# Pooled attention feeding a ResMLP block: GpSimd's v sum put behind VectorE's, scores ahead of v's product, unread products at the start, token products earlier

## The chip, the cores and the metric

The kernel runs on one core of a Trainium2 chip. The metric is device time in microseconds (us) of one execution, the median of several runs. Now and then a run falls into a slower state with a lower granted clock (381.28 us at 0.95 in one run below, where the other five took 369.5 to 371.52 us); the times and ratios compared below are of the other runs, called fast, unless a line says otherwise.

A *lead* is by how much sooner a step starts after the change than before. *Unread products* are products of a tile of zeros whose result nothing reads. Names: PE is TensorE's products and PEld its weight loads, DVE is VectorE, ACT is ScalarE, POOL is GpSimd, SP is the engine that issues most loads. L409 is line 409 of the kernel that ran. The changed kernel has some more lines at its top, so the sum of v is at L409 and L411 before and at L415 and L417 after; v's product with the selection matrix is L417 before and L423 after.

## The reference

```python
# q, k, v: (8 batches, 8 heads, 576, 64); pool = 8
k_p, v_p = mean of k, v over groups of 8 rows            # 72 rows
attn = softmax(q @ k_p.T / sqrt(64))
x = heads side by side of attn @ v_p                     # (8, 576, 512)
# ResMLP with affine steps
a1 = alpha1 * x + beta1
u  = x + lam * (w_tok @ a1)
ch = relu((alpha2 * u + beta2) @ w_ch1) @ w_ch2          # 512 -> 2048 -> 512
out = u + lam * ch
```

## The kernel before

The program is written out in order; each engine runs its own instructions in that order and waits for what it needs. The 36 chunks of 128 rows (8 batches of 4.5 chunks) form 9 blocks of four chunks for the MLP. While block n runs its MLP on TensorE, the attention of batch n + 1 is threaded between its products. The first batch has nothing to hide behind: loads, attention, token products and MLP follow each other. These parts matter here (cuts are marked):

```python
def sum_v(b, u, eng=nc.vector):              # pool v by 8: three adds, 128x512, 128x256, 128x128
    t = st1[b]["v"][u]
    for n in (4, 2):
        eng.tensor_tensor(out=t[:, :, 0:n], in0=t[:, :, 0:n], in1=t[:, :, n:2 * n], op=ALU.add)
    vs = work.tile([P, 2, D], F16, tag="v_sum", bufs=2, name="v_sum")
    eng.tensor_tensor(out=vs, in0=t[:, :, 0], in1=t[:, :, 1], op=ALU.add)
    ...
# att_V(b, u): product of the sums with a selection matrix (ps_v), then two copies into vp
# att_S(b, h): two score products (ps_sc) and their exponentials on ScalarE (ET)
# att_AV(b, h): five products with v (ps_av), reciprocal, and x written by VectorE
# att_X(b, h0, h1, eng): xs = x * lam * alpha1
# mix_T(b, c): token product of chunk c (ps_tok), then u and u_bf on VectorE
# mix_uT(key): transposes of u_bf (ps_uT), copied to u_fm by ScalarE: the MLP's input

sum_v(0, 0)                                  # first batch: VectorE sums heads 0-3 ...
att_Vrem(0, nc.scalar.copy)
sum_v(0, 1, nc.gpsimd)                       # ... and GpSimd heads 4-7, at the same time
att_S(0, 4)
att_V(0, 0, nc.vector.tensor_copy)
att_AV(0, 0)
att_S(0, 5)
att_AV(0, 1)
att_AV(0, 2)
att_X(0, 0, 2, nc.gpsimd)
att_S(0, 6)
...
def attention(b):                            # later batches: (place among the MLP's steps, what)
    ...
    for c in range(5):
        at = 25.4 + 0.8 * c if late else 25.0 + (0.8 if b % 2 else 1.0) * c
        todo.append((at, lambda c=c: mix_T(b, c)))
        if c < 4 or b % 2:
            key = (b, c) if c < 4 else (b - 1, 4)
            todo.append((at + 1.8, lambda key=key: mix_uT(key)))
# mlp_B(n, m, part), four w2 products each, stands at places 16 to 31
```

The softmax here doesn't subtract the row's maximum and nothing guards it: scores larger than these inputs give would overflow.

## Time and profile before

| | before |
|---|---|
| time, median of 3 runs | 372.29 us (372.1 to 372.67) |
| span of the profiled run | 370.5 us |
| TensorE busy | 353.9 us (95%) |
| first token product starts | 27.28 us |
| TensorE's waits after 40 us | three for u_bf, 0.8 us in all |

The page cuts the span into 40 slices of 9.26 us; a digit is the busy share in tenths. These are TensorE's and the loads' rows of the kernel before:

```profile
PE   6589999999999999999999999999999999999995
DMA  6999795049002902093107402470100002002002
```

TensorE is short of work in the first three slices alone (6, 5, 8), which are the loads, the attention and the first token products of the first batch. From there it is at 9 until the last slice. So there are two places to gain: the first 28 us, and small waits elsewhere that add to tenths of a microsecond.

### The profile page before, as it was taken

Reading aid. Unit: us, or ns where it says so; the run is one execution under the profiler, and the core shown is the slowest. Engines: PE = TensorE matmul, PEld = TensorE weight load, DVE = VectorE, ACT = ScalarE, POOL = GpSimd, SP = SyncE. Lnnn points to the kernel's source line nnn. Section 1 sums busy time; section 2 is a strip of 40 time slices with the busy share of each in tenths; the row PEclk is TensorE's granted clock in tenths of the full one; section 3 lists DMA queues with packets and bytes.
Section 4 is the critical chain, followed back from the end, with each engine's and each line's share of the span. In section 5 each row is a group of like instructions: output and inputs, shape, how many; then the busy total and the mean of one; then the engine's idle time right before and its main releaser. Section 6 shows DMA issues by size and latency. Waiting matters only on the chain.

```text
span 370.5 us, 6098 instructions
## 1 busy us (share of the span) xinstructions
PE 353.9 (95%) x2302; PEld 196.0 (53%) x2344; DVE 217.5 (59%) x426; ACT 201.9 (54%) x408; POOL 145.7 (39%) x188
## 2 busy tenths in 40 slices
PE   6589999999999999999999999999999999999995
PEld 2366655455545554455545555555455545544544
DVE  7876355773697358833885289527963687643011
ACT  3763984269614981399228932795159704712710
POOL 8955907910494038601880079105920410000000
PEclk9999999999999999999999999999999999999999
DMA  6999795049002902093107402470100002002002
GB/s 247 269 224 328 186 271 183 2 145 350 31 30 80 333 30 58 28 315 98 58 28 253 160 31 58 156 257 30 57 28 2 28 31 58 2 28 85 2 30 83
DMA packets 19575, 43.27 MB, mean 117 GB/s; under 512 B 2193, under 2 KB 4565, under 8 KB 19546
## 3 DMA queue, kind: packets, MB, share of 16 engines
q1 hardware_dynamic: 17488, 37.89, 30.2%
q0 software_dynamic: 1888, 4.86, 6.9%
q8 instruction: 18, 0.29, 0.3%
q10 hardware_dynamic: 170, 0.14, 0.2%
q14 instruction: 11, 0.09, 0.1%
HBM read 38.30 MB, written 9.44 MB: 129 GB/s over the span
## 4 chain that ended last, share of the span: by engine, by line
PE 84%; DVE 7%; ACT 3%; DMA 2%; issue 2%; SPq 1%; ACTq 0%
PE ps_h L542 32%; PE ps_ch L565 31%; PE ps_tok L511 9%; PE ps_sc L446 4%; DVE u_bf L515 3%; PE ps_av L463 2%; DVE u_sb L513 2%; DMA qk_raw<-in_k_dram 2%; PE ps_uT L526 2%; PE ps_q L362 2%; DVE v_u L409 1%; ACT wtT L284 1%; ACT Hj L547 1%; PE ps_kp L394 1%; SPq L78 1%
## 5 line engine op out<-in xcount | busy, mean ns | idle before, releaser
L542 PE MATMUL ps_h<-u_fm,w 128*128 128x512 bf16 (+1 forms) x574 | 133.2, 373 | 1.2 <-ACT u_fm L528 0.4
L565 PE MATMUL ps_ch<-w,Hj 128*128 128x512 bf16 x493 | 123.4, 379 | 1.1 <-issue 0.2
L547 ACT ACTIVATE Hj<-ps_h,bias_cols 128x512 bf16<-128x512 f32 x144 | 96.6, 690 | 36.5 <-PE ps_h L542 21.4
L542 PEld LDWEIGHTS <-w 128*128 128x128 bf16 x592 | 64.8, 114 | 47.9 <-issue 0.6
L477 POOL TENSOR_TENSOR xs<-x_tm,lamal_bc 128x512 bf16<-128x512 f32 x24 | 30.5, 1271 | 140.1 <-DVE x_tm L470 137.1
L565 PEld LDWEIGHTS <-Hj 128*128 128x128 bf16 x592 | 55.6, 98 | 48.1 <-issue 0.2
L528 ACT COPY u_fm<-ps_uT 128x512 bf16<-128x512 bf16 x36 | 21.1, 585 | 88.3 <-PE ps_uT L526 88.3
L448 ACT ACTIVATE ET<-ps_sc 128x288 f16<-128x288 f32 (+1 forms) x128 | 51.7, 487 | 15.8 <-PE ps_sc L446 15.6
L511 PE MATMUL ps_tok<-xs,wtT 128*128 128x512 bf16 (+1 forms) x197 | 48.3, 379 | 0.2
L401 DVE CAST kpT<-ps_kp 64x288 bf16<-64x288 f32 x31 | 14.1, 455 | 52.0 <-PE ps_kp L397 51.6
L572 DVE TENSOR_TENSOR u_sb<-u_sb,ps_ch 128x512 f32<-128x512 f32 (+1 forms) x37 | 24.9, 673 | 24.9 <-PE ps_ch L565 23.8
L515 DVE TENSOR_TENSOR u_bf<-u_sb,al_bc 128x512 bf16<-128x512 f32 (+1 forms) x39 | 34.4, 881 | 1.4
L571 DVE TENSOR_TENSOR ps_ch<-lam_bc,ps_ch 128x512 f32<-128x512 f32 x32 | 22.1, 692 | 20.6 <-PE ps_ch L565 20.4
L513 DVE TENSOR_TENSOR u_sb<-x_tm,ps_tok 128x512 f32<-128x512 f32 (+1 forms) x40 | 27.4, 684 | 10.5 <-PE ps_tok L511 10.0
L132 POOL TENSOR_TENSOR qk_raw<-qk_raw 128x512 f32<-128x512 f32 (+1 forms) x28 | 32.6, 1165 | 1.1
L470 DVE TENSOR_TENSOR x_tm<-ps_av,rec 128x320 f32<-128x320 f32 x64 | 31.5, 492 | 2.7
L511 PEld LDWEIGHTS <-wtT 128*128 128x128 bf16 (+1 forms) x200 | 19.3, 98 | 22.7 <-PE ps_vec L271 0.3
L468 DVE RECIPROCAL rec<-ps_av 128x5 f32<-128x5 f32 x64 | 12.3, 193 | 32.0 <-PE ps_av L466 31.9
L446 PE MATMUL ps_sc<-qT,kpT 128*128 128x288 bf16 (+1 forms) x128 | 28.8, 306 | 0.6 <-DVE kpT L401 0.5
L463 PEld LDWEIGHTS <-ET 72*128 72x128 f16 (+1 forms) x256 | 16.7, 100 | 14.2 <-DVE vp L421 0.6
L409 DVE TENSOR_TENSOR v_u<-v_u 128x512 f32<-128x512 f32 (+1 forms) x30 | 19.7, 657 | 0.8
L463 PE MATMUL ps_av<-vp,ET 72*128 72x66 f16 (+1 forms) x256 | 18.6, 196 | 0.5 <-DVE vp L421 0.4
(112 smaller groups left out, 302.6 us busy)
## 6 DMA issues: line engine op xcount, KB each, us to landing
qk_raw<-in_q_dram SPq DMA_DIRECT2D x16, 512.0 KB, 5.6
qk_raw<-in_k_dram SPq DMA_DIRECT2D x16, 512.0 KB, 7.5
v_u<-in_v_dram SPq DMA_DIRECT2D x32, 256.0 KB, 6.7
out_dram<-u_sb SPq DMA_DIRECT2D x32, 256.0 KB, 2.3
w<-in_moe_w_ch_dram POOLq DMA_DIRECT2D x2, 1024.0 KB, 11.6
w<-in_moe_w_ch_dram POOLq DMA_DIRECT2D x4, 512.0 KB, 10.8
rem_raw<-in_q_dram SPq DMA_DIRECT2D x8, 128.0 KB, 5.3
rem_raw<-in_k_dram SPq DMA_DIRECT2D x8, 128.0 KB, 5.5
```

The lines of the kernel that those rows point to most:

```text
L132: eng.tensor_tensor(out=t[:, :, 0:n], in0=t[:, :, 0:n], in1=t[:, :, n:2 * n], op=ALU.add)
L446: nc.tensor.matmul(out=ps_sc[0:n, 0:288], lhsT=kpT_pool[u][:, j, r, 72 * hh:72 * hh + n], rhs=st["qT"][u][:, h % 4, :])
L448: nc.scalar.activation(out=ET[0:n, 64 + j:64 + S + j:2], in_=ps_sc[0:n, 0:288], func=AF.Exp, bias=0.0, scale=1.0 / 64)
L463: nc.tensor.matmul(out=av[:, c, :], lhsT=ET[:, m0:m0 + 256:2], rhs=vp1)
L470: nc.vector.tensor_tensor(out=x[:, :, dd:dd + D], in0=av[:, :, 0:64], in1=rec.unsqueeze(2).to_broadcast((P, 5, D)), op=ALU.mult)
L477: eng.tensor_tensor(out=xs[:, 0:4, cols], in0=x[:, 0:4, cols], in1=lamal_bc[:, cols].unsqueeze(1).to_broadcast((P, 4, D * (h1 - h0))), op= ...
L511: nc.tensor.matmul(out=ps_tok, lhsT=wtT[0:kk, at, t0:t0 + P], rhs=xs[0:kk, sc, :], start=(sc == 0), stop=(sc == 4))
L513: nc.vector.tensor_tensor(out=s["u"][p0:p1, :], in0=st1[b]["x"][p0:p1, c, :], in1=ps_tok[p0:p1, 0:DM], op=ALU.add)
L515: eng.tensor_tensor(out=s["u_bf"][p0:p1, :], in0=s["u"][p0:p1, :], in1=al2_bc[p0:p1, :], op=ALU.mult)
L542: nc.tensor.matmul(out=ps_h[:, t0:t1], lhsT=w1_of(cc, j), rhs=u_fm[n][:, cc, t0:t1], start=(cc == 0), stop=(cc == 3))
L547: nc.scalar.activation(out=t, in_=ps_h, func=AF.Relu, bias=bias_cols[:, j:j + 1], scale=1.0)
L565: nc.tensor.matmul(out=ps, lhsT=Hj[n, j][:, 128 * m:128 * m + 128], rhs=w2_of(n, j, cols), start=(j == 0), stop=(j == NJ - 1))
```

## The change

Its intent: let VectorE sum its v without GpSimd beside it, give ScalarE two more scores to work on before v's product, raise TensorE's clock with unread products, and start the later token products a little earlier. The diff, cut to its core (`keep_warm(n)` issues n unread products; it was also moved up, and its left operand is now a part of `warm` instead of the identity):

```diff
+    warm = const.tile([P, DM], BF, tag="warm", name="warm")   # moved up
+    nc.vector.memset(warm, 0.0)                               # was GpSimd's
...
     new_batch(1)
+    keep_warm(6)
     ps_lam = broadcast(0)
     nc.scalar.copy(out=lam_bc, in_=ps_lam)
+    keep_warm(2)
     ps_lamal = broadcast(1)
...
-    keep_warm(2)
...
+    v_00 = st1[0]["v"][0]
     sum_v(0, 0)
     att_Vrem(0, nc.scalar.copy)
+    nc.gpsimd.memset(v_00[:, 0, 0, 0:1], 0.0)
     sum_v(0, 1, nc.gpsimd)
     att_S(0, 4)
+    att_S(0, 5)
     att_V(0, 0, nc.vector.tensor_copy)
     att_AV(0, 0)
-    att_S(0, 5)
     att_AV(0, 1)
+    att_S(0, 6)
+    att_X(0, 0, 2, nc.gpsimd)
     att_AV(0, 2)
-    att_X(0, 0, 2, nc.gpsimd)
-    att_S(0, 6)
+    att_S(0, 7)
     att_AV(0, 3)
     att_X(0, 2, 4, nc.gpsimd)
-    att_S(0, 7)
...
-            at = 25.4 + 0.8 * c if late else 25.0 + (0.8 if b % 2 else 1.0) * c
+            at = 25.2 + 0.8 * c if late else 24.6 + (0.8 if b % 2 else 1.0) * c
```

The memset writes one column of a tile that VectorE has finished with. Its only use is that GpSimd may write this tile only after VectorE's sum has read it, and so waits.

More of the change, by code (lines that the diff above doesn't have):

```diff
@@ L62, with keep_warm @@
     NBLK = len(chunks) // 4
+    def keep_warm(count):
+        ps = gp("ps_warm")
+        for _ in range(count):
+            nc.tensor.matmul(out=ps, lhsT=warm[:, 0:P], rhs=warm)
     st1 = {}
@@ L216 @@
     xs_pool = consts([P, 5, DM], BF, "xs", 2)
-    warm = const.tile([P, DM], BF, tag="warm", name="warm")
     b2c_bf = const.tile([P, 4], BF, tag="b2c_bf", name="b2c_bf")
@@ L245, in fill_mix @@
         nc.gpsimd.memset(wtT[:, :, S:640], 0.0)
-        nc.gpsimd.memset(warm, 0.0)
         nc.gpsimd.memset(xs_pool[1][0:64, 4, :], 0.0)
@@ L495, in chunk_of @@
         return key, st2[key]
-    def keep_warm(count):
-        ps = gp("ps_warm")
-        for _ in range(count):
-            nc.tensor.matmul(out=ps, lhsT=identity_bf, rhs=warm)
     def mix_T(b, c, eng=nc.vector):
```

## The prediction

> **What bounds the kernel now.** I read the page first (busy shares, chain of waits by engine), then TensorE's waits over the whole span, then the timeline of each engine from 10 to 28 us, and last the end of one steady block (137 to 156 us).
>
> The page, busy shares and chain by engine:
>
> ```profile
> PE 353.9 (95%) x2302; PEld 196.0 (53%) x2344; DVE 217.5 (59%) x426; ACT 201.9 (54%) x408; POOL 145.7 (39%) x188
> PE 84%; DVE 7%; ACT 3%; DMA 2%; issue 2%; SPq 1%; ACTq 0%
> ```
>
> TensorE is the bound: 353.9 of 370.5 us, so all its idle time is 16.6 us. Only that can be saved, because the change removes no work that is read later. TensorE's waits, the whole span (waiter, released by: us in total, times, longest):
>
> ```profile
> PE ps_v L417 <- DVE v_sum L411: 3.5, 1, 3.5
> PE ps_bc L260 <- DMA vecs<-in_moe_lam_dram: 2.7, 1, 2.7
> PE ps_uT L526 <- DVE u_bf L515: 0.8, 3, 0.3
> PE ps_rs L293 <- ACT wtT L284: 0.6, 1, 0.6
> ```
>
> The largest is the target: v's product of the first batch (line 417) waits 3.5 us for VectorE's sum of v. The 0.8 us in three pieces is the only recorded wait of size after 40 us. The timeline there, VectorE first, then GpSimd (start, duration, both us):
>
> ```profile
> 14.84 2.57 DVE L409 TENSOR_TENSOR v_u<-v_u 128x512 f32<-128x512 f32 x1
> ...
> 15.56 2.44 POOL L409 TENSOR_TENSOR v_u<-v_u 128x512 f32<-128x512 f32 x2
> 18.07 0.52 POOL L411 TENSOR_TENSOR v_sum<-v_u 128x128 f16<-128x128 f32 x1
> ```
>
> and the same three VectorE instructions in the second batch, with GpSimd quiet, then ScalarE's first exponential after its long pause:
>
> ```profile
> 47.17 1.15 DVE L409 TENSOR_TENSOR v_u<-v_u 128x512 f32<-128x512 f32 x2
> 48.36 0.29 DVE L411 TENSOR_TENSOR v_sum<-v_u 128x128 f16<-128x128 f32 x1
> ...
> 20.19 0.83 ACT L448 ACTIVATE ET<-ps_sc 128x288 f16<-128x288 f32 x2 [3.50 <-PE ps_sc L446]
> ```
>
> The reader is to see three things. VectorE's first-heads sum runs from 14.84 to 18.75 us, 3.9 us, while GpSimd sums the second heads; alone it takes 48.65 - 47.17 = 1.5 us. GpSimd is hardly hurt (1.30 us for its 128x512, against 1.27 us for its other 128x512 adds of two inputs). And ScalarE idles 3.5 us, because the scores of head 5 stand behind the first product with v in TensorE's order.
>
> **What the Trainium skill says.** "SBUF — State Buffer", section "Who interferes with whom": a VectorE instruction with two SBUF inputs contends with a GpSimd instruction that reads SBUF, the later one blocked until the first is done. The trace agrees on the contention (2.57 us against 0.69 us for a 128x512 sum), but not simply on who was first: VectorE's add started 0.72 us ahead of GpSimd's. In those 0.72 us GpSimd issued the second load of w1 (14.79 to 15.56), so descriptor writing may hold the port too. "GPSIMD Engine Reference", section "Engine selection": two-input elementwise work is about twice as slow on GpSimd; here 1.30 against 0.69 us. "TensorE: Matmul & The Clock Gate", Part 1: TensorE runs at half clock until about 3.4 us of sustained work. The page's clock row says 9 all along, yet four products with v take 0.22 us in the chain at 20.39 and 0.12 us at 53.24, so the early stage does run at half rate.
>
> **The change, part by part.**
>
> 1. GpSimd waits for VectorE (a one-column memset of the tile that VectorE sums). VectorE's sum then costs 1.5 us from 14.8: done at 16.3 if the load's descriptors do not block it, and at about 15.56 + 1.5 = 17.05 if they do. I take the middle, 16.7, against 18.75: 2.05 us earlier. GpSimd's sum starts only then and takes 1.3 + 0.75 + 0.5 = 2.5 us, plus 0.1 for the memset: done at 19.3, against 18.6 before. Before, that result was first used at 22.2, so it had slack.
>
> 2. Scores of head 5 go ahead of v's product, and those of heads 6 and 7 one product earlier. ScalarE does head 5's exponentials (0.83 us) in its pause, after 16.7. Before, from VectorE's sum (18.75) to head 6's exponential (21.30) took 2.55 us, with head 5's 0.83 us of ScalarE inside; now about 1.4 us.
>
> 3. From there two chains run to the first token product, which started at 27.28. ScalarE's: four exponentials 1.5, copies of v 0.5, then four copies of the transposed token weights and the row sums (22.68 to 27.10 before with the copies of v, 4.4 us): 16.7 + 1.4 + 1.5 + 4.4 + 0.2 = 24.2. GpSimd's: its sum at 19.3, then three products x times lam*alpha, each 1.27 + 0.45 us, 5.2 us: 24.5, and some 0.2 for VectorE's own one beside it. So the first token product goes to about 24.6: **2.7 us earlier**; 3.1 with the early VectorE end, 2.3 with the late one. GpSimd becomes the tighter of the two.
>
> 4. Unread products at the beginning: six of 128x512, then two between the two broadcasts, in place of two later ones; the clear of their input goes from GpSimd (0.53 us) to VectorE. TensorE waited 2.7 us for lam then, so the six lie mostly in idle time (6 x 0.43 = 2.6 us cold, from about 1.2 to 3.8), and delay the first broadcast by 1.1 us at most. The second-half k load, used by VectorE at 11.28, sets the pace until 14.8. I count **0 to -0.2 us**: faster k products on the chain, and a warm array for the first products with v, which the GpSimd chain mostly hides.
>
> 5. mix_T of later batches at 24.6 for 25.0 (25.2 for 25.4 in the first block). The order of instructions shows where this lands. In even batches nothing but the token products moves; the last transposes keep their place. In the first block the last transposes keep their place too. In batches 3, 5 and 7 the last transpose moves ahead of one group of w2 products (0.86 us), which before filled the time in which VectorE finished. The end of such a block:
>
> ```profile
> 152.32 0.69 DVE L513 TENSOR_TENSOR u_sb<-x_tm,ps_tok 64x512 f32<-64x512 f32 x1
> 153.04 1.06 DVE L515 TENSOR_TENSOR u_bf<-u_sb,al_bc 64x512 bf16<-64x512 f32 x1
> ...
> 154.16 0.40 PE L526 MATMUL ps_uT<-identity_bf,u_bf 128*128 128x128 bf16 x4 [0.29 <-DVE u_bf L515]
> ```
>
> VectorE is busy almost without a gap from 144.38 to 154.10, and was held by TensorE only 0.34 us at its start. If the token products start 0.86 us earlier, VectorE gains at most 0.33, and perhaps nothing, because its first u_bf then still waits for GpSimd's k sum that began at 144.38. TensorE is 0.86 us earlier at the last transpose and waits: 0.29 + 0.86 - 0.33 = 0.8 to 1.15 us in place of 0.29. That **costs 0.5 to 0.9 us** in each of batches 3 and 5, and some 0.2 in batch 7, where GpSimd has no next batch: together about 1.5 us.
>
> Sum: -2.7 - 0.1 + 1.5 = -1.3 us; 372.29 - 1.3 = **371.0 us**.
>
> **Rivals.**
> - *The serial GpSimd becomes the bound of the start.* Its sum now follows VectorE's, and its three products follow. For it: the chain above ends later than ScalarE's. Against a large loss: before, it also worked without a break from 21.57 to 26.56 and the first token product started 0.7 us later. If VectorE is blocked by the descriptors, the gain at the start falls to 2.3 us: 371.4 us.
> - *The steady part gains.* Earlier token products may give VectorE a head start that removes the three waits (0.8 us), if GpSimd's contention falls differently. Then 372.29 - 2.8 - 0.8 = 368.7. Against it: VectorE is already full there, and the changed order takes its filler away.
> - *The gain at the start is swallowed by loads.* The DMA share is about 1.0 from 9 to 37 us, so starting the second batch's loads earlier does not make them land earlier. Against it: GpSimd's casts and sums of the second batch, and VectorE's v sum at 41.35, show no wait for a DMA. The last v of that batch is issued at 33 and lands some 6.6 us later, its first half by 37.6, and VectorE would want that at 38.6. If it does bite, up to 1 us is lost: 372.
> - *The early unread products get in the way*: if the array is still cold at the broadcasts, the second ends at 8.8 instead of 7.6 us and the first exponentials come 0.5 us later; ScalarE's pause of 3.5 us takes that up.
>
> **Range and chances.** Start gain 1.9 to 3.4 us, steady loss -0.5 to 2.2 us: a change between -3.9 and +0.3 at the corners; both are unlikely to be at their ends at once, so 369.4 to 372.1 us should hold it 8 times in 10. The 2% bound is 7.4 us. All idle time that the change touches is smaller, and nothing in it adds 7 us of work, so within 2% is nearly certain.
>
> **What would show it right or wrong.** Right: TensorE's wait at line 417 falls from 3.5 to about 1.5 us; VectorE's three v sums take 1.5 to 2.3 us and GpSimd's start after them; ScalarE's pause ahead of head 6 falls under 1 us; the first token product starts near 24.6; TensorE's waits for u_bf grow from 0.8 to about 2.2 us, in batches 3 and 5. Wrong: VectorE's sum still takes 2.5 us or more with GpSimd still (then the load's descriptors, or the data's arrival, held it and not GpSimd's sum), a first token product after 25.5, a DMA wait at the second batch, or u_bf waits that vanish.

## The result and the profile after

The changed kernel took 371.49 us (median of 4 runs, 371.15 to 371.97) against 372.2 us of the kernel before (4 runs). The ratio is 0.9983, with a 95% interval of 0.9964 to 1.0003. A ratio here is the mean time of one kernel's fast runs over that of the other's of the same rounds, so it is not quite the ratio of the two medians. That is 0.7 us by the medians; since the interval includes 1, no gain is shown by the times.

The page of the changed kernel, busy shares and chain by engine:

```profile
PE 357.2 (97%) x2308; PEld 196.4 (53%) x2350; DVE 217.1 (59%) x427; ACT 201.8 (55%) x408; POOL 147.3 (40%) x188
PE 89%; DVE 5%; ACT 4%; issue 1%; DVEq 0%
```

TensorE's busy time rose by 3.3 us although the span fell: unread products, 4.16 us of it after and 1.45 before, count as busy. A busy share is no measure of use.

TensorE's waits in the changed kernel, over the span (waiter, released by: us in total, times, longest):

```profile
PE ps_uT L526 <- DVE u_bf L515: 2.1, 5, 0.6
PE ps_warm L68 <- DVE warm L160: 1.3, 1, 1.3
PE ps_sc L452 <- ACT qT L389: 0.8, 1, 0.8
PE ps_rs L299 <- ACT wtT L290: 0.6, 1, 0.6
PE ps_v L423 <- DVE v_sum L417: 0.6, 1, 0.6
```

The large wait for VectorE's v sum is gone: 0.6 us for 3.5. The wait for u_bf, which had been 0.8 us in three pieces, is now the largest. The timeline of the changed kernel's first batch (start, duration, engine, what; in brackets the idle time before it and what ended it):

```profile
15.32 1.15 DVE L415 TENSOR_TENSOR v_u<-v_u 128x512 f32<-128x512 f32 x2
...
16.51 0.29 DVE L417 TENSOR_TENSOR v_sum<-v_u 128x128 f16<-128x128 f32 x1
...
16.86 0.10 POOL L613 MEMSET v_u<- 128x1 f32 x1 [1.34 <-DVE v_sum L417]
16.96 2.07 POOL L415 TENSOR_TENSOR v_u<-v_u 128x512 f32<-128x512 f32 x2
...
18.59 1.60 ACT L454 ACTIVATE ET<-ps_sc 72x288 f16<-72x288 f32 x4 [0.37 <-PE ps_sc L452]
...
24.79 3.41 PE L511 MATMUL ps_tok<-xs,wtT 128*128 128x512 bf16 x15
```

VectorE's three adds take 1.48 us (15.32 to 16.80) where they took 3.9. GpSimd's start after them. ScalarE pauses 0.37 us ahead of head 6 where it had paused 3.5 us ahead of head 5. The first token product starts at 24.79 us, 2.5 us earlier. What it waited for at the end, from the chain that ended last in the changed kernel:

```profile
20.62 1.96 ACT wtT L290 x3
...
23.04 0.70 ACT wtT L290
...
23.78 0.44 PE ps_rs L299 x5
```

These are ScalarE's copies of the transposed token weights and the products behind them, to which TensorE adds an unread product that ends at 24.69 us. VectorE's own product with lam*alpha ends at 24.65 us. GpSimd's third one of 128 rows had ended at 24.09 us; from 19.5 us on no GpSimd instruction stands in this chain.

The end of the block of batch 3 in the changed kernel, TensorE's timeline:

```profile
149.09 0.39 PE L526 MATMUL ps_uT<-identity_bf,u_bf 128*128 128x128 bf16 x4
149.87 0.40 PE L526 MATMUL ps_uT<-identity_bf,u_bf 128*128 128x128 bf16 x4 [0.40 <-DVE u_bf L515]
150.32 0.81 PE L565 MATMUL ps_ch<-w,Hj 128*128 128x512 bf16 x3
151.69 0.40 PE L526 MATMUL ps_uT<-identity_bf,u_bf 128*128 128x128 bf16 x4 [0.55 <-DVE u_bf L515]
151.92 1.89 PE L565 MATMUL ps_ch<-w,Hj 128*128 128x512 bf16 x8
153.65 2.54 PE L542 MATMUL ps_h<-u_fm,w 128*128 128x512 bf16 x11
```

Two transposes now wait, 0.95 us together, and eight w2 products (1.7 us) that could have filled the time stand behind the last of them. Before, the order was: a w2 group, the third transpose, a group, the fourth, a group, the last, one more group. So the fourth and the last have each overtaken one group of four. The last u_bf of the same block in the changed kernel, which the last transpose waits for:

```profile
150.57 1.06 DVE L515 TENSOR_TENSOR u_bf<-u_sb,al_bc 64x512 bf16<-64x512 f32 x1
```

VectorE ends it at 151.63 us, against 154.10 before: 2.47 us earlier, which is the lead that the block began with. The earlier token products have not made VectorE finish any sooner. The last transpose follows it at once in both kernels, but from its start to the next block it was 1.10 us before (154.16 to 155.26, one group) and is 1.96 us now (151.69 to 153.65, two groups): 0.86 us more.

Where the gain of the start goes can be read off by lining up the first w1 product (L542) of each block in the two traces:

| block starts, us | 1 | 2 | 3 | 4 | 5 | 6 | 7 | end of span |
|---|---|---|---|---|---|---|---|---|
| before | 77.10 | 115.94 | 155.26 | 194.11 | 233.42 | 272.28 | 311.12 | 370.5 |
| after | 74.60 | 113.47 | 153.65 | 192.52 | 232.69 | 271.56 | 310.56 | 369.9 |
| lead | 2.50 | 2.47 | 1.61 | 1.59 | 0.73 | 0.72 | 0.56 | 0.6 |

The lead of 2.5 us falls by 0.86 us at the end of batch 3's block, by 0.86 us at the end of batch 5's, and by 0.16 us at batch 7's. It does not change in the blocks of the even batches.

### The profile page after: what moved, and what is told of

The parts are those of the page before. It is cut to its first block, busy times and chain, and to the rows that moved or that the text cites. A ratio compares the mean times of both kernels' runs of the same rounds, so it can differ in the third digit from the quotient of the medians.

```text
span 369.9 us, 6111 instructions
## 1 busy us (share of the span) xinstructions
PE 357.2 (97%) x2308; PEld 196.4 (53%) x2350; DVE 217.1 (59%) x427; ACT 201.8 (55%) x408; POOL 147.3 (40%) x188
## 4 chain that ended last, share of the span: by engine, by line
PE 89%; DVE 5%; ACT 4%; issue 1%; DVEq 0%
PE ps_h L542 32%; PE ps_ch L565 30%; PE ps_tok L511 11%; PE ps_sc L452 4%; PE ps_av L469 2%; PE ps_q L368 2%; DVE u_bf L515 2%; PE ps_uT L526 2%; DVE u_sb L513 1%; PE ps_warm L68 1%; PE ps_bc L266 1%; ACT wtT L290 1%; ACT qT L372 1%; DVE xs L483 1%; ACT Hj L547 1%
## 5 line engine op out<-in xcount | busy, mean ns | idle before, releaser
L542 PE MATMUL ps_h<-u_fm,w 128*128 128x512 bf16 (+1 forms) x574 | 133.7, 373 | 1.4 <-ACT u_fm L528 0.4
L542 PEld LDWEIGHTS <-w 128*128 128x128 bf16 x592 | 64.8, 114 | 47.9 <-issue 0.6
L571 DVE TENSOR_TENSOR ps_ch<-lam_bc,ps_ch 128x512 f32<-128x512 f32 x32 | 22.1, 691 | 24.8 <-PE ps_ch L565 24.7
L515 DVE TENSOR_TENSOR u_bf<-u_sb,al_bc 128x512 bf16<-128x512 f32 (+1 forms) x39 | 35.2, 902 | 1.4
L511 PEld LDWEIGHTS <-wtT 128*128 128x128 bf16 (+1 forms) x200 | 18.3, 98 | 21.4 <-DVE xs L483 2.6
L469 PEld LDWEIGHTS <-ET 72*128 72x128 f16 (+1 forms) x256 | 16.7, 100 | 14.1 <-DVE vp L427 0.6
L415 DVE TENSOR_TENSOR v_u<-v_u 128x512 f32<-128x512 f32 (+1 forms) x30 | 18.6, 621 | 1.5 <-DMA v_u<-in_v_dram 0.7
```

Of the source, the lines that this page charges most:

```text
L469: nc.tensor.matmul(out=av[:, c, :], lhsT=ET[:, m0:m0 + 256:2], rhs=vp1)
L511: nc.tensor.matmul(out=ps_tok, lhsT=wtT[0:kk, at, t0:t0 + P], rhs=xs[0:kk, sc, :], start=(sc == 0), stop=(sc == 4))
L515: eng.tensor_tensor(out=s["u_bf"][p0:p1, :], in0=s["u"][p0:p1, :], in1=al2_bc[p0:p1, :], op=ALU.mult)
L542: nc.tensor.matmul(out=ps_h[:, t0:t1], lhsT=w1_of(cc, j), rhs=u_fm[n][:, cc, t0:t1], start=(cc == 0), stop=(cc == 3))
```

## The experiments

Twelve runs were made, in three groups of four; each group had its own runs of the kernel before on the same chip (medians 371.98, 372.59 and 372.44 us). All results were correct. Each ratio is to the kernel before. By the 2% rule all twelve are "same"; the differences below are smaller and rest on the intervals and the traces.

| label | what it is | median, us | ratio (95%) |
|---|---|---|---|
| start_1and2 | before + GpSimd's wait + order of scores | 369.76 | 0.9945 (0.9928 to 0.9962) |
| mix_only | before + earlier token products | 374.3 | 1.0061 (1.0045 to 1.0078) |
| warm_only | before + early unread products | 373.02 | 1.0021 (1.0005 to 1.0037) |
| after_mix_back | changed kernel, token products put back | 370.03 | 0.9950 (0.9936 to 0.9963) |
| part1_wait | before + GpSimd's wait | 369.8 | 0.9936 (0.9917 to 0.9955) |
| part2_order | before + order of scores | 371.96 | 0.9994 (0.9976 to 1.0013) |
| after_uT_kept | changed kernel, transposes put back | 370.04 (fast runs; 370.28 with the slow one) | 0.9945 (0.9923 to 0.9967) |
| after_warm_ones | changed kernel, ones in the unread products | 372.35 | 0.9997 (0.9980 to 1.0014) |
| start_again | start_1and2 once more | 369.82 | 0.9929 (0.9911 to 0.9947) |
| uT4_deferred | start_1and2, last transpose later | 368.26 | 0.9900 (0.9874 to 0.9927) |
| no_unread | start_1and2 without any unread product | 369.79 | 0.9928 (0.9906 to 0.9951) |
| after_warm_long | changed kernel, 16 early products for 6 | 372.44 | 1.0000 (0.9977 to 1.0024) |

### The reordered first batch alone (start_1and2, start_again)

```diff
 # on the kernel before
+    v_00 = st1[0]["v"][0]
     sum_v(0, 0)
     att_Vrem(0, nc.scalar.copy)
+    nc.gpsimd.memset(v_00[:, 0, 0, 0:1], 0.0)
     sum_v(0, 1, nc.gpsimd)
 # and att_S(0, 5) to att_S(0, 7), att_X(0, 0, 2) in the order of the changed kernel
```

> The kernel before with only the reordered first batch: GpSimd waits for VectorE's v sum, and the scores of head 5 to 7 go earlier; no early unread products, token products of later batches where they were. My theory: the start gives 2.5 to 3 us and the early unread products gave nothing, so the first token product starts at 24.2 to 25.0 us (27.28 before), u_bf waits of TensorE stay at 0.8 us, and the time is 369.3 to 369.8 us. VectorE's v sum starts near 14.84 us, while GpSimd still issues the loads of w1 (until 15.56): if descriptor writing blocks it, the three v sums take about 2.2 us; if only GpSimd's own sum did, 1.5 us. Rival: the early unread products are what made the start faster: then the first token product is at 26 us or later and the time at 371 us or more.

It took 369.76 us, and 369.82 us when it ran again: 2.0 and 2.6 us under the kernel before by the ratios. The u_bf waits stayed at 0.8 us. The first token product started at 25.08 us, at the slow edge of what I expected, because the whole start was late in this run: VectorE's adds began at 15.61 us, since the load of k landed later. It settles whether the writing of load descriptors holds VectorE up. The timeline of start_1and2:

```profile
15.56 0.77 POOL L317 DMA_DIRECT2D w<-in_moe_w_ch_dram  x1
15.61 1.15 DVE L409 TENSOR_TENSOR v_u<-v_u 128x512 f32<-128x512 f32 x2
```

VectorE's first two adds took 1.15 us, which is their time alone, although GpSimd issued the second load of w1 through 0.72 us of it. Descriptor writing did not block them.

For the second time, as a base:

> The kernel with only the reordered first batch once more, as the base for the two next runs on the same chip: 2.0 to 2.6 us under the kernel before, u_bf waits 0.8 us in three pieces.

That held: 0.9929, and u_bf waits of 0.8 us in three pieces. In this trace, unlike the changed kernel's, the chain to the first token product runs through GpSimd's sum of v (16.33 to 19.04 us).

### The earlier token products alone (mix_only)

```diff
 # on the kernel before
-            at = 25.4 + 0.8 * c if late else 25.0 + (0.8 if b % 2 else 1.0) * c
+            at = 25.2 + 0.8 * c if late else 24.6 + (0.8 if b % 2 else 1.0) * c
```

> The kernel before with only the token products of later batches earlier (24.6 and 25.2 for 25.0 and 25.4). My theory: the start is as before (first token product at 27.3 us), TensorE's waits for u_bf grow from 0.8 to about 2.1 us, and the time grows by 1.7 to 2.0 us, to about 374 us. Rival: the earlier token products are neutral or gain, and the missing gain of the change was lost elsewhere: 371.5 to 372.3 us with u_bf waits under 1 us.

The time rose by 0.61%, 2.3 us, somewhat more than expected, and the interval (1.7 to 2.9 us) holds the 1.9 us that the table of leads shows. TensorE's waits in mix_only have the line of the changed kernel:

```profile
PE ps_v L417 <- DVE v_sum L411: 2.9, 1, 2.9
...
PE ps_uT L526 <- DVE u_bf L515: 2.1, 5, 0.6
```

The first token product started at 27.55 us (27.28 before). The loss is made by this part, without help from the start.

### The early unread products alone (warm_only)

```diff
 # on the kernel before
+    keep_warm(6)
     ps_lam = broadcast(0)
     nc.scalar.copy(out=lam_bc, in_=ps_lam)
+    keep_warm(2)
     ps_lamal = broadcast(1)
...
-    keep_warm(2)
```

> The kernel before with only the early unread products (six and two at the beginning in place of two later). My theory: the second broadcast ends 1.4 us later, the first exponentials 0.8 us later and VectorE's v sum 0.3 to 0.5 us later; the array stays cold, so the first token product moves to 27.6 to 27.8 us and the time grows by 0.3 to 0.5 us, to about 372.6 us. Rival: they warm the array by 10 us (score products start to start 0.12 us apart rather than 0.24 us), and the first token product is at 27.0 us or earlier.

The time rose by 0.21% (0.2 to 1.4 us), and the first token product started at 27.96 us. TensorE's timeline of warm_only shows why nothing was gained:

```profile
8.97 1.03 PE L368 MATMUL ps_q<-identity_bf,q_bf 128*128 128x128 bf16 x8
...
11.27 1.35 PE L452 MATMUL ps_sc<-qT,kpT 128*72 128x288 bf16 x4 [0.81 <-ACT qT L389]
```

Eight transposes took 1.03 us, as they did in the kernel before, so the array was at half rate still; they started at 8.97 us, against 7.54 before. The scores then waited 0.81 us for ScalarE's copy of q. How much the early products cost in the whole is not settled. In this trace the second half of k was also late (VectorE waited for it until 12.02 us, 11.28 before). The time rose by 0.21%, but after_mix_back, which has them, and start_1and2, which has not, differ by only 0.05% on the same chip.

### Token products put back (after_mix_back)

```diff
 # on the changed kernel
-            at = 25.2 + 0.8 * c if late else 24.6 + (0.8 if b % 2 else 1.0) * c
+            at = 25.4 + 0.8 * c if late else 25.0 + (0.8 if b % 2 else 1.0) * c
```

> The changed kernel with the token products of later batches put back where they were. My theory: the first token product stays at 24.8 us, the u_bf waits fall back from 2.1 to 0.8 us, and the time is 1.7 to 2.0 us under the changed kernel's, about 369.6 us. Rival: the gain of the start is given back anyhow in the steady part (loads, or VectorE): 371 us or more.

370.03 us, a ratio of 0.9950, with u_bf waits of 0.8 us. The first token product started at 25.15 us, not at 24.8. So with the gain of the start in place the loss of the token products can be taken back, and the start's gain arrives at the end.

### GpSimd's wait alone (part1_wait) and the order of scores alone (part2_order)

```diff
 # part1_wait: on the kernel before
+    nc.gpsimd.memset(v_00[:, 0, 0, 0:1], 0.0)
     sum_v(0, 1, nc.gpsimd)
 # part2_order: on the kernel before, only att_S(0, 5) to att_S(0, 7) and att_X(0, 0, 2) moved
```

> The kernel before with GpSimd's wait alone; scores of head 5 stay behind the first product with v. My theory: VectorE's three v sums take 1.5 us instead of 3.9, the product with v starts some 2 us earlier, but head 5's exponentials still come after it, so the first token product moves by about 1.7 us only (25.4 to 25.7 us against 27.28) and the time by -1.5 to -1.9 us, near 370.3 us. Rival: the wait does nothing by itself, because GpSimd's sum, started later, holds the second heads' product: first token product after 26.5 us, 371.5 us or more.

It gained more than I expected: 0.64%, 2.4 us by the ratio, and the first token product started at 24.52 us. The timeline of VectorE in part1_wait:

```profile
14.49 1.15 DVE L409 TENSOR_TENSOR v_u<-v_u 128x512 f32<-128x512 f32 x2
15.68 0.29 DVE L411 TENSOR_TENSOR v_sum<-v_u 128x128 f16<-128x128 f32 x1
```

The adds took 1.48 us, 2.4 us less than before. From their end (15.97) to the first token product (24.52) it was 8.55 us, against 8.53 us before (18.75 to 27.28). So the chain behind the sum is as long as it was, and the whole of what VectorE saves reaches the token products.

> The kernel before with the scores of heads 5, 6 and 7 earlier, but GpSimd and VectorE still summing side by side. My theory: TensorE's wait for VectorE's v sum stays near 3 us, head 5's exponentials (0.83 us) move into ScalarE's pause, and the first token product comes 0.8 to 1.1 us earlier (26.2 to 26.5 us), the time -0.7 to -1.0 us, near 371.1 us. Rival: the order alone gives nothing, since GpSimd's products with lam*alpha or VectorE end last: within 0.3 us of the kernel before.

The ratio is 0.9994: no gain is shown. Of the expected 0.7 to 1.0 us (0.9981 to 0.9973) the smaller is inside the interval, the larger outside. The trace has the first token product at 26.26 us, as expected, but 0.65 us of this 1.0 us comes from VectorE's sum, which ended earlier although GpSimd still worked beside it. ScalarE's timeline in part2_order:

```profile
16.12 1.49 ACT L448 ACTIVATE ET<-ps_sc 72x288 f16<-72x288 f32 x4
19.89 1.60 ACT L448 ACTIVATE ET<-ps_sc 72x288 f16<-72x288 f32 x4 [2.28 <-PE ps_sc L446]
```

Head 5's exponentials did move ahead of the pause, and the chain from the end of VectorE's sum (18.10) to the token product is 8.16 us, 0.4 us shorter. That is less than the 0.83 us moved. In the changed kernel and in start_1and2 it is 7.99 us; in start_again, the same program as start_1and2, 8.57 us, and in after_mix_back 8.42 us. So the order is worth 0 to 0.55 us in single traces, and the times don't resolve it: part1_wait alone is as fast as start_1and2.

### Transposes put back (after_uT_kept)

```diff
 # on the changed kernel
-                todo.append((at + 1.8, lambda key=key: mix_uT(key)))
+                todo.append((at + (2.0 if late else 2.2), lambda key=key: mix_uT(key)))
```

> The changed kernel with its early token products, but each transpose of u put back where it was (offset 2.2 and 2.0 for 1.8). My theory: the loss comes from the last transpose having overtaken its filler of four w2 products, so the u_bf waits fall from 2.1 to under 1 us and the time to 369.5 to 370.0 us, as with everything put back. Rival: the early token products themselves cost, by making VectorE and GpSimd collide more: u_bf waits stay above 1.5 us, or the waits move elsewhere, 371 us or more.

The ratio of the fast runs is 0.9945, the same as with everything put back. So early token products do no harm by themselves that the time shows; it was the place of the transposes. This run puts the fourth and the last back together and doesn't separate them. The profile of this kernel fell in the slow state (381 us, granted clock 0.95), so its waits are not read here, and the expected fall of the u_bf waits is not shown directly.

### The last transpose later still (uT4_deferred)

```diff
 # on start_1and2
-                todo.append((at + 1.8, lambda key=key: mix_uT(key)))
+                todo.append((at + 1.8 if c < 4 else 31.5, lambda key=key: mix_uT(key)))
```

In an odd batch the fifth chunk, (b - 1, 4), belongs to a later block than the next one. Its transpose may stand behind the last w2 products.

> The reordered first batch alone, and in odd batches the last transpose of u goes behind the last group of w2 products (it is not needed by the next block). My theory: the place of the last transpose against its filler is what makes the u_bf waits, so the three waits (0.8 us) vanish and the time falls by 0.6 to 0.9 us against the run of the reordered first batch alone. Rival: the waits move to the copies of u or to the next block's first products, and the time stays within 0.2 us.

368.26 us, a ratio of 0.9900, against 0.9929 of start_again on the same chip: about 1.1 us better, somewhat more than expected, though the two intervals overlap. The traces agree: the starts of the blocks gain 0.32, 0.48 and 0.47 us on start_again at the ends of the blocks of batches 1, 3 and 5, and nothing at the end of batch 7's. The list of TensorE's waits has no line for u_bf any more, and TensorE's busy time from 80 to 240 us rose from 159.36 of 160 us (start_again) to 159.94. This version is faster than both kernels, by 1.0% than the kernel before.

### What the unread products do (after_warm_ones, after_warm_long, no_unread)

```diff
 # after_warm_ones: on the changed kernel
-    nc.vector.memset(warm, 0.0)
+    nc.vector.memset(warm, 1.0)
 # after_warm_long: on the changed kernel
-    keep_warm(6)
+    keep_warm(16)
 # no_unread: on start_1and2, both remaining pairs removed
-    keep_warm(2)
...
-    keep_warm(2)
```

> The changed kernel with ones instead of zeros in the unread products. In the changed kernel TensorE was busy from 1.3 to 10 us and yet the products until 20 us ran at half rate. Theory A: zero operands don't count as activity for the clock; with ones the second broadcast takes 1.0 instead of 2.0 us, score products stand 0.12 instead of 0.24 us apart from about 6 us on, and the first token product starts by 24.5 us. Theory B: the value doesn't matter, the early stage is cold for another reason (these forms of products, or gaps): everything within the spread of the changed kernel, first token product 24.6 to 25.1 us, 371.5 us.

The value did not matter to the clock there: the broadcasts took 2.07 us each and the first scores stood as far apart as with zeros. The time was that of the kernel before (0.9997); the first token product started at 25.36 us, outside what either theory named, with VectorE's sum late by 0.16 us.

> The changed kernel with 16 unread products at the beginning in place of six, 6.9 us at half rate. Theory A: sustained full-size products release the clock within 3.4 to 6.8 us, so that the later of them stand 0.22 us apart instead of 0.43 and the score products after them 0.12 us instead of 0.24 us apart; the broadcasts end later, near 10 us, and the first token product is at 25 us or a little later. Theory B: nothing in this stage releases the clock: all 16 stand 0.43 us apart, the broadcasts end at 13 us, the first scores come 4 us later, and the time grows by 2 to 4 us.

TensorE's timeline of after_warm_long:

```profile
1.32 5.32 PE L68 MATMUL ps_warm<-warm 128*128 128x512 bf16 x16 [1.32 <-DVE warm L160]
6.57 1.12 PE L266 MATMUL ps_bc<-vecs,ones_row 1*128 1x512 f32 x2
...
9.21 0.62 PE L368 MATMUL ps_q<-identity_bf,q_bf 128*128 128x128 bf16 x8
...
12.21 1.06 PE L368 MATMUL ps_q<-identity_bf,q_bf 128*128 128x128 bf16 x8
```

Theory A held as to the clock: sixteen products in 5.3 us cannot all have stood 0.43 us apart (6.9 us), the broadcasts took 1.1 us for 2.07, and eight transposes 0.62 us for 1.03. But at 12.21 us the same eight transposes took 1.06 us again, and the kernel's time is that of the kernel before (1.0000). The rate was won and lost again before the part of the start where it could help, and that part waits for loads, VectorE and ScalarE anyway.

> The reordered first batch alone with no unread products at all (both pairs removed). My theory: unread products do nothing for the clock in the first 20 us, and the pair ahead of the token products only fills a wait for ScalarE: within 0.3 us of the reordered first batch alone, first token product 7.9 to 8.4 us after the product with v, as there. Rival: they keep the array's clock up, and the token products then start cold: TensorE's 15 token products take 6 us in place of 3.4 and the time grows by 1 us or more.

369.79 us and 0.9928, as start_again (0.9929). The 15 token products took 3.41 us with or without unread products ahead of them. They do nothing that the time shows. The trace has the first token product at 23.58 us, 8.0 us after the sum's end, as expected, but 1.3 us earlier than start_again's (24.84). That run took 368.56 us, the fastest of the six; whether the missing products or chance made its start so early, one trace doesn't tell.

## Why the prediction was right

The time on record was 371.0 us with a range of 369.4 to 372.1; 371.49 us was measured. By its steps:

1. **VectorE's sum.** It said 1.5 us if descriptors do not block, 2.2 us if they do, and took the middle. It is 1.48 us, and start_1and2 shows the adds at full speed beside a load being issued. Half of this hedge was wrong. The sum's end, 16.7 in the prediction and 16.80 in the trace, came out right partly by luck: the adds also started 0.48 us later than before (15.32 for 14.84). That GpSimd was hardly hurt before holds for its first add alone (1.30 us, 1.27 alone); its second took 1.06 us, and 0.73 alone.
2. **The order of scores.** Counted as part of a step from 2.55 to 1.4 us. The changed kernel needed 1.8 us there (16.80 to 18.59), and the order alone shortened its chain by 0.4 us in one trace. This term was too large; part1_wait shows that GpSimd's wait brings nearly all of the start's gain.
3. **The two chains to the first token product.** 24.6 us predicted, 24.79 measured; GpSimd's sum ended at 19.57 (19.3 predicted). But which chain is the tighter was wrong: GpSimd's third product of 128 rows was done at 24.09, while ScalarE's and TensorE's chain, predicted for 24.2, and VectorE's own product ended near 24.7. That the number fits is in part luck. ScalarE paused 0.37 us (under 1 predicted). TensorE's wait for v's sum is 0.6 us, not 1.5: its products ahead of this one now end 0.96 us later (16.28 for 15.32), 0.58 us because they start later and 0.38 us by head 5's scores, which I had forgotten.
4. **Early unread products.** Predicted 0 to -0.2 us. They did not raise the clock, and no gain is seen: two comparisons put their cost at 0.05% and 0.21% (0.2 and 0.8 us), of which the first is within the noise. The prediction's own rival came true: with the array still cold the second broadcast ended at 9.03 us (7.60 before) and the first exponentials started at 11.70 us (10.91 before).
5. **The later token products.** This step carries the result. Predicted: the last transpose overtakes a group of w2 products in batches 3, 5 and 7, at 0.5 to 0.9 us each for the first two and 0.2 us for the third, and nothing in even batches or in the first block. The leads fall by 0.86, 0.86 and 0.16 us, and nowhere else; the u_bf waits are 2.1 us (2.2 predicted), 1.0 us of it in each of the two blocks. The upper end was the right one: VectorE gained nothing. The prediction overlooked that the fourth transpose overtakes a group too (0.40 us of the wait). After_uT_kept shows the cause: with the transposes alone back in place the loss is gone.

Sum by the traces: -2.5 at the start, +1.9 later, -0.6 us; predicted -1.3. The rivals: the steady part did not gain. A wait for a load in the second batch, named as a sign of being wrong, did appear (VectorE waited 0.72 us for v, until 39.54 us), but the lead is the same after it (2.50 and 2.47 us), so it cost nothing. The prediction forecast no clear change, and the time shows none.

## What to carry to other kernels

When a change moves several things, line up the starts of the same step in both traces: a lead of 2.5 us that falls by 0.86 us at two places names the part that gives the gain away, which the total time hides. An instruction of an in-order engine that waits costs what stands behind it, so before moving one earlier, ask what it overtakes: here four products (0.86 us) that had filled the wait were lost, and the head start brought nothing. Two engines that sum side by side can hurt the one that matters: together the two sums took 3.9 us before (14.84 to 18.75) and 4.25 us one after the other (15.32 to 19.57), but the half that TensorE waits for is done after 1.48 us. The one-column memset that makes GpSimd wait is worth 2.4 us.

## What the Trainium skill lacked or had wrong

- "TensorE: Matmul & The Clock Gate", Part 1, gives some 3.4 us of sustained work as what releases the clock. After_warm_long agrees: the single records of its 16 products start 0.43 us apart from 1.32 to 4.71 us and 0.22 us apart from 4.97 us on, so the release came after 3.4 to 3.7 us. On which work counts, the page says in Part 4 only that transposes in transpose mode do not count as busy in the same way. It lacks products with one row of fp32: in the changed kernel TensorE was busy without a recorded gap from 1.32 to 10.4 us (six full-size products, then mainly one-row broadcasts and transposes) and the scores at 11.26 us still ran at half rate. That the one-row products don't count either is my guess; no run separates them.
- The same page says that the clock is throttled again after one idle window of about 3.4 us. In after_warm_long eight transposes took 0.62 us at 9.21 and 1.06 us at 12.21, with a recorded wait of TensorE of only 1.0 us between. This speaks against the page only if the broadcast and the transposes after the last full-size unread product (7.85 us) count as work; that is open.
- "SBUF — State Buffer", section "Who interferes with whom", infers that a two-input sum on VectorE and descriptor writing do not meet, since they need different sides of the shared ports. Start_1and2 supports it: two adds in 1.15 us beside a load issue of 0.77 us, as fast as alone.
- The same section says that issue order decides who blocks. In the kernel before VectorE's add started 0.72 us ahead of GpSimd's by the records, alone it takes 0.69 us, and yet it took 2.57 us; in part2_order, with the same distance, 1.17 us. In the kernel before, mix_only and warm_only VectorE's add ended 0.56 us after GpSimd's first add did (17.41 and 16.85 us in the kernel before), as if it had been held for all of that add. Why is open; recorded starts on GpSimd may be late.
